# The same tasks in another hand-written order: a fused S5 scan and MLP kernel on one Trainium2 core

## The chip, the core and the metric

The kernel runs on one core of one Trainium2 chip (trn2). The metric is device time in microseconds (us), from start to end of one execution. Kernels are compared by the median of several runs on the same chip.

The core has a matrix engine (TensorE, called PE in the profile, with its weight loads as PEld), a vector engine (VectorE, DVE), an activation engine (ScalarE, ACT), a general engine (GpSimd, POOL) and a queue that only issues transfers here (SyncE, SP). Each engine takes its instructions strictly in the order in which the program lists them. An instruction that has to wait for a semaphore therefore holds up everything behind it on its engine.

## The reference

Input `x` is one sequence of 2048 rows with 448 channels, bf16. It is normalised twice (a layernorm of a layernorm feeds the MLP), goes through a complex diagonal recurrence (S5) and through an MLP of width 1792, and both meet in a gate:

```python
xn = layernorm(x)                                        # over the 448 channels
# A: S5. 448 complex states, one decay Lam_bar per state
Lam_bar = exp(exp(log_dt) * (Lambda_re + 1j * Lambda_im))
Bu      = xn @ B_bar.T ;  h[t] = Lam_bar * h[t-1] + Bu[t]     # t = 0..2047
s       = 2 * real(h @ C.T) + xn * Dskip
# B: MLP on the layernorm of xn, gate
m   = gelu_tanh(layernorm(xn) @ w1 + b1) @ w2 + b2
out = x + s * silu(m)
```

## The kernel before

**Tiling.** The 2048 rows are cut into four groups of 512 (`NG = 4`, g = 0 to 3), each of two blocks of 256 rows; a block holds its even and odd rows as two halves of 128 partitions. Two steps of the recurrence are folded into one, so that the scan of a group runs over 256 positions, and the two outputs of a pair come from two prepared matrices, `CZ` and `CQ`.

**What each group does.** Statistics and normalisation (`ln_stats`, L399; `ln_scale`, L478 to L488; `ln_apply`, L499 on DVE or L500 on ACT) give `xn` for the scan and `xm` for the MLP. Both are turned by transposing transfers that SP issues (L83); only the first group's `xm` is transposed on PE (L460) and copied from PSUM (L417). The first MLP layer `mm1_run` (matmuls L801) writes pairs of PSUM banks, and ACT's Gelu (L805) empties them: there are three pairs, so PE can be at most three pairs ahead of ACT. The second layer `mm2` (L828) needs the Gelu outputs; DVE adds its bias (L831). The scan's input `bu` (L729) goes to ACT or DVE (L417), then `ssm` on DVE: products (L744 to L748), scans (L753, L755), products back (L771 to L775) into `h_sb`. The outputs `ym` (L871, L874, L877) use one PSUM bank, number 7, for groups 0 to 2, which DVE must read (L885 or L888, or L883) before the next `ym` may write it. The result is added and stored (L891, SP).

**What runs once.** At the start a few tiny vectors of the S5 parameters are worked out in some eighty small operations on 128x4 or 128x16 elements (L534 to L592; a sine polynomial of ten chained steps, L545 to L551), then tables of sines (`tables`: DVE L624 to L631, ACT L640), then the mixed matrices `LB` and `CQ`, `CZ` (`combine`, L658 to L661) and `M0` (L712, L697, and their PSUM reads L417, L718, L705). PE begins with matmuls on constants whose result nobody reads (`dummies`, L422). ACT loads four function tables after its first (L443, L614, L618, L614 again near the end).

**What sets the order.** The body of the kernel only records tasks: 633 of them, each with an engine, its reads and its writes. Some are recorded with two possible engines (`either`, `small`, `copy`, `combine`, `ln_apply`). Then `Plan.emit` takes two lists of numbers written out at the top of the file:

```python
for k in SECOND:
    self.tasks[k].choose(1)
order = [self.tasks[k] for k in ORDER]
```

`SECOND` names the tasks that go to their second engine, and `ORDER` the sequence in which all tasks are handed to the engines. The waits are derived from reads and writes after that, so any order that respects them computes the same thing. No scheduler and no due times stand behind the lists when the program is built: the order on each engine is what `ORDER` says.

Of the kernel before, what the change touches and what calls it, by code (L numbers as in the profile page):

```python
# [159 lines left out]


ORDER = [int(k) for k in """
# [17 lines left out]
""".split()]  # L180
SECOND = [int(k) for k in """
45 53 54 61 63 66 69 74 76 83 112 130 133 158 160 162 163 165 177 184 185 187 189 190 220 222 224 226 228 230 238 248 249 258 266 268 331 362 364 365
384 400 401 436 447 468 480 482 487 491 499 501 502 504 510 528 529 609 612 627
""".split()]


# [834 lines left out]
```

## Time and profile before

| | |
|---|---|
| time of the kernel before | 153.37 us, median of 3 runs (153.15 to 153.41) |
| span of the profiled execution, first to last instruction | 151.8 us |
| time of the three runs beyond that span | 1.6 us |
| busy: PE / DVE / ACT / POOL | 147.1 / 127.6 / 99.0 / 42.1 us |
| instructions: PE / DVE / ACT / POOL | 1127 / 267 / 183 / 101 |
| granted TensorE clock | 1.00 |

The profile gives no time of its own beside the span: what lies around the profiled execution is taken as the difference of the median and the span. In rows of the timeline the first number is the start in us from the span's start, the second the length of the piece, then engine, source line, operation, what is written and read, and how many instructions were merged; the bracket behind a row gives the idle time before it and what ended it. A row of a group of instructions has "busy us, mean ns of one | idle us before". A row of the windows gives the stretch, its length, and the busy time of each engine with its number of instructions.

### The profile page before, as it was taken

What the parts mean: (1) busy time and instruction counts of PE and PEld (TensorE: products, weight loads), DVE (VectorE), ACT (ScalarE), POOL (GpSimd) and SP (SyncE); (2) the same over time, 40 slices, a digit from 0 to 9 for tenths busy, and PEclk for the clock granted to TensorE, in tenths of its full rate; (3) what the DMA queues carried; (4) which work ended last, traced back from release to release, by engine and by line L of the source; (5) the groups of instructions that cost most, each with busy time, mean ns of one, the idle gap of its engine ahead of it and who ended that gap; (6) DMA issues with size and microseconds to landing.
All of it is one profiled execution on the core that took longest, in us unless ns stands there. A gap on an engine that the chain in (4) does not pass through costs nothing.

```text
span 151.8 us, 2974 instructions
## 1 busy us (share of the span) xinstructions
PE 147.1 (97%) x1127; PEld 86.6 (57%) x1127; DVE 127.6 (84%) x267; ACT 99.0 (65%) x183; POOL 42.1 (28%) x101
## 2 busy tenths in 40 slices
PE   7899999999999999999999999999999999999992
PEld 7785755454566577545444556764454666555551
DVE  2874999999978979999999996379968726999984
ACT  3888996988789559997898610463579834067400
POOL 5376827153020920010456006200072031000201
PEclk9999999999999999999999999999999999999999
DMA  4999999989997300700003032610331001100022
GB/s 116 262 305 390 266 202 138 219 152 133 165 261 180 65 0 0 138 0 4 0 0 63 4 60 45 154 60 4 60 101 23 0 4 57 64 0 0 4 84 98
DMA packets 31236, 14.73 MB, mean 97 GB/s; under 512 B 24752, under 2 KB 30774, under 8 KB 31222
## 3 DMA queue, kind: packets, MB, share of 16 engines
q1 hardware_dynamic: 30912, 14.26, 41.8%
q0 software_dynamic: 160, 0.23, 1.0%
q8 instruction: 9, 0.15, 0.4%
q10 hardware_dynamic: 150, 0.05, 0.1%
q14 instruction: 5, 0.04, 0.1%
HBM read 6.89 MB, written 1.84 MB: 57 GB/s over the span
## 4 chain that ended last, share of the span: by engine, by line
PE 80%; DVE 9%; DMA 4%; SPq 4%; issue 2%
PE psum L828 23%; PE psum L801 22%; PE psum L729 14%; PE psum L871 13%; DMA x_all<-in_A_x_dram 4%; PE psum L874 4%; SPq L84 4%; PE psum L712 3%; DVE xn_sb L499 2%; DVE lnst L399 1%; DVE s_w L628 1%; PE psum L877 1%; DVE o L831 1%; PE psum L697 1%; DVE tmp L891 1%
## 5 line engine op out<-in xcount | busy, mean ns | idle before, releaser
L801 PE MATMUL psum<-xn2T,w_sb 64*128 64x512 bf16 (+1 forms) x462 | 44.6, 345 | 0.3 <-ACT xn2T L417 0.2
L828 PE MATMUL psum<-w_sb,gT 128*128 128x448 bf16 x224 | 44.5, 353 | 0.2 <-DVE o L831 0.2
L805 ACT ACTIVATE gT<-psum,b1f 128x512 bf16<-128x512 f32 (+1 forms) x66 | 35.9, 625 | 10.4 <-PE psum L801 10.2
L801 PEld LDWEIGHTS psum<-xn2T,w_sb 64*128 64x128 bf16 x462 | 24.1, 109 | 19.8 <-ACT gT L805 2.3
L828 PEld LDWEIGHTS psum<-w_sb,gT 128*128 128x128 bf16 x224 | 21.5, 98 | 20.7 <-DVE o L831 0.6
L417 ACT ACTIVATE u_sb<-psum 128x512 bf16<-128x512 f32 (+2 forms) x22 | 10.5, 478 | 23.0 <-PE psum L729 22.7
L729 PE MATMUL psum<-xnT,BT 128*128 128x256 bf16 x196 | 24.0, 273 | 0.0
L729 PEld LDWEIGHTS psum<-xnT,BT 128*128 128x128 bf16 x196 | 18.9, 98 | 5.4 <-issue 1.1
L891 POOL TENSOR_TENSOR tmp<-t,x_all 128x448 bf16<-128x448 bf16 x5 | 5.2, 1032 | 33.1 <-DVE t L888 30.7
L753 DVE TENSOR_TENSOR_SCAN s_w<-dk,vs 128x774 f32<-128x774 f32 x8 | 14.0, 1760 | 0.1
L500 ACT ACTIVATE xn_sb<-x_all,lnw 128x448 bf16<-128x448 bf16 (+2 forms) x21 | 13.0, 662 | 1.2 <-DVE xn_sb L499 1.1
L417 ACT ACTIVATE vs<-s_w 64x256 bf16<-64x256 f32 (+2 forms) x16 | 10.9, 681 | 2.6 <-DVE s_w L753 1.5
L871 PE MATMUL psum<-CZ,h_sb 128*128 128x448 bf16 x56 | 11.9, 352 | 0.0
L871 PE MATMUL psum<-CQ,h_sb 128*128 128x448 bf16 (+2 forms) x54 | 10.5, 332 | 0.0
L399 DVE BATCH_NORM_STATS2 lnst<-x_all 128x6 f32<-128x448 bf16 x12 | 7.1, 617 | 3.4 <-DMA x_all<-in_A_x_dram 3.4
L831 DVE TENSOR_TENSOR o<-psum,b2bc 128x448 f32<-128x448 f32 x16 | 9.7, 614 | 0.2
L871 PEld LDWEIGHTS psum<-CZ,h_sb 128*128 128x128 bf16 x56 | 5.4, 98 | 4.7 <-DVE lnmv L405 0.4
L871 PEld LDWEIGHTS psum<-CQ,h_sb 128*128 128x128 bf16 x54 | 5.1, 98 | 4.0 <-DVE t L885 0.4
L874 PE MATMUL psum<-M,xnT 128*128 128x448 bf16 x32 | 7.4, 352 | 0.0
L480 POOL TENSOR_TENSOR lnw<-lnw,mhalf 128x8 f32<-128x8 f32 x3 | 7.2, 2404 | 0.3
L883 DVE TENSOR_TENSOR Cr<-psum,xd 128x448 f32<-128x448 f32 x7 | 4.3, 620 | 3.5 <-PE psum L877 3.4
L499 DVE TENSOR_SCALAR xn_sb<-x_all,lnw 128x448 bf16<-128x448 bf16 (+2 forms) x19 | 6.9, 396 | 0.0
(160 smaller groups left out, 189.1 us busy)
## 6 DMA issues: line engine op xcount, KB each, us to landing
out_dram<-tmp SPq DMA_DIRECT2D x7, 224.0 KB, 2.0
x_all<-in_A_x_dram SPq DMA_DIRECT2D x3, 448.0 KB, 4.0
w_sb<-in_B_w_dram SPq DMA_DIRECT2D x3, 448.0 KB, 8.4
w_sb<-in_B_w_dram SPq DMA_DIRECT2D x3, 384.0 KB, 4.8
vs<-in_A_C_re_dram SPq DMA_DIRECT2D x1, 392.0 KB, 11.6
Bn<-in_A_B_im_dram SPq DMA_DIRECT2D x1, 336.0 KB, 10.2
Bn<-in_A_B_re_dram SPq DMA_DIRECT2D x1, 336.0 KB, 10.5
vs<-in_A_C_im_dram SPq DMA_DIRECT2D x1, 336.0 KB, 10.8
```

Source lines behind the costliest of these rows:

```text
L399: dve([lambda e, b=b, par=par, q=q: e.bn_stats(lnst[:, q, :], x_all[:, 2 * g + b, par, :])], [f"x{2 * g + b}"] , [f"st{q}"], 0.62, prio)
L417: kb.either(("act", [lambda e, o=o, i=i: e.activation(o, i, ACT.Copy) for o, i in pairs]), ("dve", [lambda e, o=o, i=i: e.tensor_copy(o, i ...
L499: on = [("dve", [lambda e, o=o, i=i: e.tensor_scalar(o, i, rs, nb, op0=ALU.mult, op1=ALU.add) for o, i in parts], 0.4, 0.12), ("act", [lam ...
L500: ("act", [lambda e, o=o, i=i: e.activation(o, i, ACT.Identity, bias=nb, scale=rs) for o, i in parts], 0.75, 0.2)]
L729: fns = [lambda e, r=r, m=m, d=d: e.matmul(psum[:, 4, r * NK:(r + 1) * NK], BT[:, m, d, :], xnT[:, gx, d, :], start=(d == 0), stop=(d == 6 ...
L753: dve(lambda e, so=so, vi=vi: e.tensor_tensor_scan(so, dk[:].rearrange("p i c -> p (i c)"), vi, 0.0, ALU.mult, ALU.add), ["v", "vl", "dk", ...
L801: return lambda e: e.matmul(view(bk[k]), w1_sb[rows, d, fcol(2 * j + k)], rhs[rows, d, :, :], start=not second and n == 0, stop=second and ...
L805: act([lambda e, k=k: e.activation(gT[:, gb, 2 * j + k, :].rearrange("p (r c) -> p r c", r=2)[:, :, cols], view(bk[k]), ACT.Gelu_apprx_tan ...
L828: fns = [lambda e, fi=fi: e.matmul(psum[:, bk, 0:D], gT[:, gb, fi, q * 128:(q + 1) * 128], w2_sb[:, fi, :], start=(fi == 0), stop=(fi == N ...
L831: dve(lambda e: e.tensor_tensor(o2[:, fb, :], psum[:, bk, 0:D], b2bc[:], ALU.add), [f"ps{bk}", "b2bc"], [f"oo{fb}"], 0.62, prio - 76)
L871: fns = [lambda e, k=k: e.matmul(psum[:, bk, c0:c1], h_sb[:, hb, k, k0:k0 + 128], cm[:, k, c0:c1], start=(k == 0), stop=False) for k in ra ...
L874: fns += [lambda e, d=d: e.matmul(psum[:, bk, c0:c1], xnT[:, gx, d, xs], M0[:, d, c0:c1], start=False, stop=(d == 3)) for d in range(4)]
```

## The change

Two lists are replaced and nothing else. `ORDER` holds the same 633 numbers in another sequence. `SECOND` goes from 60 to 78 entries. SP's 23 loads at the start keep their order.

Counted by engine, 46 tasks with 65 instructions come to DVE: 30 from POOL (43 instructions: most of the parameter arithmetic, among it the wrap L542 to L544 and the ten steps of the sine polynomial, two `De` products L610, a few small steps of the scan's carry L764 to L769, an `xd` product L847 and four result additions L891) and 16 from ACT (22 instructions: the copy of the first transposed half L417, normalisations L500, PSUM copies L417 of `bu` and `M0`, one product L658, and two copies L417 of the last but one scan). Twenty tasks with 22 instructions leave DVE: 11 to POOL (small ones, `xd` products and two result additions) and 9 to ACT (the absolute value L631, which becomes an Abs at L630, normalisations and PSUM copies). DVE's program grows from 267 to 310 instructions, ACT's shrinks by 11 and POOL's by 32.

Of the new sequence, engine by engine:

- PE: thirteen of the constant matmuls now stand together ahead of the second set of transposes (L460) instead of around it. Six matmuls of the first `mm2` (L828) stand among the first group's L801, ahead of its last five pieces; before they followed them. Four `M0` and `bu` pieces and two `mm2` of group 1 change places; two `mm2` of group 2 change places; one `ym` of group 2 goes ahead of an `mm2` of group 3.
- DVE: the parameter steps taken over stand between the first normalisations, the PSUM copies of the transposed second block and the statistics of group 1 (L399). Two of the four L628 pieces stand ahead of the normalisation of group 1 instead of behind it. From there on, DVE's tasks are interleaved differently throughout.
- ACT: the Abs (L630) stands ahead of the last three Gelu pairs of group 0.
- SP: the two transposes of `xm` of group 1 are exchanged, and three of the four transposes of `Cr` stand ahead of those of `xn`.

```diff
 ORDER = [int(k) for k in """
-0 13 19 47 9 16 18 20 14 1 94 26 17 95 91 27 92 21 15 24 48 4 96 12 108 93 90 109 97 104 103 25 105 99 22 98 49 50 55 5 51 65 106 2 110 100 111 107 29
-101 112 30 56 28 52 114 23 54 32 53 131 57 117 128 31 118 113 121 170 115 33 46 132 168 133 129 39 130 34 66 171 253 250 102 119 155 40 123 251 252
...
+47 16 9 13 19 0 24 18 17 15 20 14 10 4 26 1 2 25 27 94 21 95 91 96 22 48 92 108 29 93 99 109 49 90 30 50 104 55 103 97 32 65 106 56 3 110 105 5 111 66
+100 8 33 12 98 107 101 112 51 46 114 28 52 102 113 54 64 23 39 118 128 53 131 117 40 57 115 171 119 155 41 58 132 42 129 169 116 31 121 38 67 170 123
...
 SECOND = [int(k) for k in """
-45 53 54 61 63 66 69 74 76 83 112 130 133 158 160 162 163 165 177 184 185 187 189 190 220 222 224 226 228 230 238 248 249 258 266 268 331 362 364 365
-384 400 401 436 447 468 480 482 487 491 499 501 502 504 510 528 529 609 612 627
+45 51 53 54 57 58 60 62 63 64 66 67 69 70 71 72 73 74 75 76 77 78 79 83 84 86 107 112 130 133 158 162 184 185 186 188 190 220 222 224 228 230 238 244
+248 258 263 265 266 334 345 352 353 354 361 362 364 376 379 400 402 403 449 450 468 469 480 482 487 495 502 516 525 526 572 612 619 627
```

30 rows, old and new, of the table ORDER are left out of this document.

## The prediction

> **What bounds the kernel now.** I read the page first: busy times, the slices, the shares of the chain.
>
> ```profile
> PE 147.1 (97%) x1127; PEld 86.6 (57%) x1127; DVE 127.6 (84%) x267; ACT 99.0 (65%) x183; POOL 42.1 (28%) x101
> ...
> PE   7899999999999999999999999999999999999992
> ...
> DVE  2874999999978979999999996379968726999984
> ...
> PE 80%; DVE 9%; DMA 4%; SPq 4%; issue 2%
> ```
>
> PE has no pause in any slice between the first microseconds and the last ones, and holds 80% of the chain. DVE is the second: full through most of the first two thirds. So there are two questions. Where does the new order let PE start or pack better, and where does it make PE wait for DVE, which gets 43 instructions more? PE's own timeline, in its groups:
>
> ```profile
> 0.83 2.93 PE L422 MATMUL psum<-const-bfloat16-1.0 128*128 128x128 bf16 x26 [0.83 <-PEq L1006]
> ...
> 6.85 2.50 PE L801 MATMUL psum<-xn2T,w_sb 64*128 64x256 bf16 x42 [0.19 <-ACT xn2T L417]
> ...
> 9.84 9.26 PE L801 MATMUL psum<-xn2T,w_sb 64*128 64x256 bf16 x126
> 19.03 8.12 PE L828 MATMUL psum<-w_sb,gT 128*128 128x448 bf16 x42
> 27.33 2.82 PE L828 MATMUL psum<-w_sb,gT 128*128 128x448 bf16 x14 [0.18 <-DVE o L831]
> 30.08 10.11 PE L801 MATMUL psum<-xn2T,w_sb 64*128 64x512 bf16 x90
> ...
> 79.62 1.06 PE L801 MATMUL psum<-xn2T,w_sb 64*128 64x512 bf16 x8
> 80.61 1.31 PE L871 MATMUL psum<-CQ,h_sb 128*128 128x448 bf16 x6
> ...
> 141.92 1.30 PE L871 MATMUL psum<-CQ,h_sb 128*128 128x448 bf16 x6
> ```
>
> Little is left to win. The one group that runs below its rate is the 126 matmuls at 9.84: by the code 28 have 512 columns, which take 10.11/90 = 0.112 us each in group 1, and 98 have 256, by width 0.056. That makes 8.6 us against 9.26. So 0.6 us are waits for Gelu, hidden in "busy"; the 42 before (2.50 against 2.35) hide 0.15, and 0.18 stands at 27.33: a reserve of 0.9 to 1.0.
>
> **What DVE has to carry.** The windows between three milestones: the last normalisation for group 1's MLP, the last `CQ`, and the first `ym` result (L885).
>
> ```profile
> 0.00:22.79 22.79, 21.13 (x254) 15.58 (x255) 16.17 (x60) 18.60 (x42) 12.81 (x47) 1.00 0.94 257
> 22.79:47.05 24.26, 24.08 (x180) 12.62 (x178) 22.52 (x57) 20.03 (x32) 7.35 (x22) 1.00 1.06 182
> 47.05:80.35 33.30, 33.30 (x250) 19.28 (x247) 31.77 (x60) 27.15 (x53) 9.44 (x15) 1.00 0.17 33
> ```
>
> DVE is idle 6.6, 1.7 and 1.5 us in these. The moved operations are priced by their twins, in the timelines of POOL and of DVE and in the groups by form:
>
> ```profile
> 14.30 0.21 POOL L545 TENSOR_SCALAR ang<-ang 128x16 f32<-128x16 f32 x1
> ...
> 17.95 0.22 POOL L551 TENSOR_TENSOR ang<-ang 128x16 f32<-128x16 f32 x1
> ```
>
> ```profile
> 17.65 0.16 DVE L478 TENSOR_SCALAR lnw<-lnmv 128x4 f32<-128x4 f32 x1
> ...
> 19.92 0.17 DVE L488 SCALAR_TENSOR_TENSOR lnw<-lnmv,lnw 128x8 f32<-128x8 f32 x1
> ```
>
> ```profile
> L891 POOL TENSOR_TENSOR tmp<-t,x_all 128x448 bf16<-128x448 bf16 x5 | 5.2, 1032 | 33.1 <-DVE t L888 30.7 <-DMA out_dram<-tmp 2.4
> ```
>
> ```profile
> L891 DVE TENSOR_TENSOR tmp<-t,x_all 128x448 bf16<-128x448 bf16 x10 | 3.8, 386 | 0.1
> ```
>
> The sine polynomial is ten chained steps, 3.9 us on POOL (first and last row). DVE's own ten-step chain (L478 to L488) takes 2.44 us, so I take 2.4 for it there. Other small chained steps cost 0.15 to 0.17, a result addition 0.39 instead of 1.03. Over the kernel this brings about 17 us to DVE and takes 6 to 7 away, so its busy time should end near 138 us, of a span near 155.
>
> **Part 1, the start: a gain of 0.6.** The first L801 start about 0.35 us later, for two reasons: the thirteen constant matmuls stand ahead of the second transposes, and the copy of that half goes to DVE behind the statistics. On the other hand six L828 (8.12/42 = 0.19 each, 1.2 us in all) now run inside the stretch where PE waits for Gelu. They fill the reserve of about 1.0, which less the 0.35 leaves 0.6: I take the end of the first group's `mm2` at 29.5 instead of 30.1. Bounds: 0.9 gained, 0.4 lost.
>
> **Part 2, the second Gelu table: a loss of 1.4.** DVE's timeline at the start, ACT's groups, ACT's timeline:
>
> ```profile
> 0.88 0.17 DVE L323 MEMSET dk<- 4x128 uint32 x1 [0.88 <-PEq L1006]
> 2.89 0.63 DVE L431 BATCH_NORM_STATS2 lnst<-x_all 128x6 f32<-128x448 bf16 x1 [1.85 <-DMA x_all<-in_A_x_dram]
> ```
>
> ```profile
> L833 ACT ACTIVATE g_sb<-o 128x448 bf16<-128x448 f32 x8 | 4.3, 571 | 3.1 <-DVE o L831 3.1
> L614 ACT ACT_TABLE_LOAD x2 | 2.6, 1283 | 0.1
> L640 ACT ACTIVATE WT<-s_w,sgn 128x256 bf16<-128x256 f32 (+1 forms) x3 | 2.2, 718 | 0.1
> L640 ACT ACTIVATE WT<-s_w 128x768 bf16<-128x768 f32 x2 | 1.7, 843 | 0.9 <-DVE s_w L631 0.9
> ...
> L658 ACT ACTIVATE tmp<-Bn,cw 128x448 f32<-128x448 bf16 x1 | 0.7, 669 | 0.0
> ```
>
> ```profile
> 19.37 2.30 ACT L805 ACTIVATE gT<-psum,b1f 128x256 bf16<-128x256 f32 x6
> ...
> 32.94 3.58 ACT L805 ACTIVATE gT<-psum,b1f 128x512 bf16<-128x512 f32 x6
> ```
>
> Up to the last normalisation for group 1, DVE had 16.2 us of work. The new list adds 4.8 of moved steps and 1.8 of pieces pulled ahead (two L628, one L831), and loses 0.7: 22.1. Some 2.7 us at the very start cannot be filled (0.88 and 1.85), so it ends at 25 instead of 22.8. The L628 that the Abs needs stands 5.3 us of work earlier, at 19.5. In the new ACT list everything behind the Abs waits for that, and then runs in a row: Abs 1.2 (a 768-wide table takes 0.84, by width 1.12 for 1024), three Gelu pairs 2.4, two normalisation pieces 1.2 (an estimate; a whole one takes less than a Silu and a half), table 1.3, four Silu 2.3, `tmp` 0.7, five sine tables 3.9, table 1.3: 14.3, and 0.1 between them. The second Gelu set is ready at 33.9 instead of 32.9, although PE comes earlier. PE has 42 matmuls until it needs its first banks back: 29.5 + 42 x 0.112 = 34.2. It gets them at 33.9 + 1.3 = 35.2, and once more about 0.3 late in the next rotation. PE loses 1.3 to 1.4 here, and stands 0.8 behind the old order. Bounds: 0 (if ACT keeps to its old times) and 2.5 (if DVE reaches that L628 a microsecond later).
>
> The transposes of group 1 hide (SP's timeline, and the table of transfers with its median time to landing):
>
> ```profile
> 21.67 3.21 SPq L83 DMA_TRANSPOSE xn2T<-xn_sb  x2
> ```
>
> ```profile
> xn2T<-xn_sb SPq DMA_TRANSPOSE x6, 3.2
> ```
>
> SP issues them at about 24.5 and 26 instead of 21.7 and 23.3, and they land 3.2 us (the median) later, near 29.2, where PE asks at 29.5. The cover is thin: without it they cost up to a microsecond, which is in the range.
>
> **Part 3, `M0` of the third column: a loss of 0.5.** The timelines of DVE and PE:
>
> ```profile
> 62.96 0.28 DVE L718 TENSOR_TENSOR M<-psum,s_w 128x128 bf16<-128x128 f32 x1
> ```
>
> ```profile
> 63.94 0.94 PE L697 MATMUL psum<-CQ,Bn 128*64 128x448 bf16 x7
> ```
>
> Before, DVE freed the bank at 63.24, 0.7 us ahead of L697. In the new list that L718 stands behind the first scan, two normalisations that came from ACT and a `tmp`. I take 0.5 of wait, between 0 and 1.5.
>
> **Part 4, the first `ym`: a loss of 1.4.** It writes bank 7, and the next `ym` has to wait for DVE's L885.
>
> ```profile
> 46.96 0.68 DVE L661 SCALAR_TENSOR_TENSOR CQ<-Cr,cw,tmp 128x448 bf16<-128x448 bf16 x1
> ...
> 79.73 0.62 DVE L885 SCALAR_TENSOR_TENSOR t<-psum,g_sb 128x448 bf16<-128x448 f32 x1
> ```
>
> From the last `CQ` to L885, DVE was busy 31.8 of 33.3 us. The new list adds 4.2 (a `bu` copy, two normalisations, `M0` and carry pieces, a `tmp`) and 1.5 pulled ahead of it (among it an L831), and takes 2.4 away: 35.1. With the same 1.5 of waits, and `CQ` at 46.9 as before (three microseconds more work, but DVE's early idle time is filled), L885 ends at 83.5. PE, 1.3 late by then, asks at 80.6 + 1.3 = 81.9, so it waits 1.6; I take 1.4, since a later PE also gives DVE's waits back in part. Bounds 0 and 3.
>
> **Part 5, the last scan: a loss of 0.5.**
>
> ```profile
> 141.37 0.29 DVE L775 TENSOR_TENSOR h_sb<-pa 128x256 bf16<-128x256 bf16 x1
> ```
>
> Its last piece ends at 141.66, 0.26 us before PE uses it at 141.92. Between L744 and this piece the new list puts 0.8 us more work (an L888, an L891, an L883 come in, an L836 and an L891 go out). That passes the margin by 0.5. The last results behind PE keep their length.
>
> **The sum.** -0.6 + 1.4 + 0.5 + 1.4 + 0.5 = 3.2 us, on a profiled span of 151.8: 155.0. The three runs' median lies 1.6 above that span; with the same surroundings, 153.37 + 3.2 = 156.6.
>
> **Rivals.** *The waits hide (152.7).* Parts 2 to 5 are all differences between DVE or ACT times that I add up and a need of PE. If DVE works its mixed list off about 2 us faster by each milestone, they vanish and part 1 is left: 153.37 - 0.6. For it: a small DVE step that waits for nothing before it may take less than the 0.16 I gave it. Against it: the added work is 5.9 us up to the first milestone and 3.3 from the second to the third, and the idle time of the two later windows only 3.2 together. Chance 0.12.
>
> *DVE's debt lands on `M0` (159.6).* In the new PE list the first `M0` follows its `mm2` directly, without a `bu` between, so `CQ` is wanted about 1.5 us sooner. If DVE does not fill its early idle time and `CQ` ends at 50 instead of 47, PE waits 2 to 3 us there more, and part 4 is unchanged: 156.6 + 3. For it speaks that DVE is full from 22.8 on (22.5 of 24.3). Chance 0.2.
>
> *PE starts at half its rate (157.5).* The first 26 constant matmuls take 2.93/26 = 0.113 us each, twice what 128 columns cost later (two 64-row L801 of 256 columns run side by side in 2 x 0.060, so 128 columns of the whole array cost 0.06). In the new list PE has nothing to do between the parameter matmuls and the first transposes, about half a microsecond (an estimate from the places in the lists), just when the rate changed. If it changes only after the thirteen others, the start of L801 moves 0.9 us: 17 matmuls of 128 columns at 0.053 more each. [...] Chance 0.15.
>
> *No change to be seen*, by chance of the terms: 0.03.
>
> **How the numbers follow.** The forecast has 0.5, the rivals 0.12, 0.2, 0.15 and 0.03. A measurement of this kernel can tell about 0.2% (0.3 us) from no change. Faster 0.12, same 0.03, slower 0.85. The range leaves out the fast rival and what lies above the slow one: 153.3 (parts 3 to 5 gone and part 2 at half, 153.37 - 0.6 + 0.7) to 160.0.
>
> **What would show it.** DVE busy 136 to 140, POOL near 30. The Gelu group after L618 starts 0.5 to 2 us later than 32.94, and the 43rd L801 of group 1 waits for it. PE shows idle or stretched groups before L697 and between the first L874 and the second L871. A first group of L828 that ends before 30 shows part 1 right. I am wrong if PE's groups from 40 to 140 keep their old distances, or if the largest wait stands where I see none, above all at group 1's transposes.

## The result: 1.7% slower, and the profile after

| | before | after |
|---|---|---|
| time, median of 4 runs each | 153.39 us (153.15 to 153.68) | 155.88 us (155.80 to 155.95) |
| ratio, with its 95% interval | | 1.0167 (1.0152 to 1.0182) |
| span of the profiled execution | 151.8 us | 154.1 us |

The change costs 2.5 us, 2.3 of them in the two spans. The runs of one kernel can lie at two levels, as 4 of the 17 runs of the kernel before that were taken beside e11_best did (154.8 to 155.1, the others 153.1 to 153.6), and no run of that upper level of the kernel before was traced. The forecast was 156.6, between 153.3 and 160.0. The total lies in that range. Its make-up was not right, as the page of the changed kernel begins to show (busy times, the slices of PE and of DVE, the shares of the chain):

```profile
PE 147.9 (96%) x1127; PEld 88.3 (57%) x1127; DVE 136.0 (88%) x310; ACT 92.8 (60%) x172; POOL 31.7 (21%) x69
...
PE   7799999999999999999999999999999899999992
...
DVE  2799998799997999999999899779999946999984
...
PE 55%; DVE 29%; ACT 6%; POOL 4%; issue 3%; DMA 1%; DVEq 0%; ACTq 0%
```

DVE now holds 29% of the chain instead of 9%, and its busy time of 136.0 is what the new list was said to bring. PE has a second weak slice at the start and one that ends at 123 us. PE's timeline gives the places:

```profile
4.92 0.61 PE L460 MATMUL psum<-ident,xn_sb 128*128 128x128 bf16 x4 [0.63 <-DVE xn_sb L453]
5.32 1.59 PE L422 MATMUL psum<-const-bfloat16-1.0 128*128 128x128 bf16 x13
6.70 0.63 PE L460 MATMUL psum<-ident,xn_sb 128*128 128x128 bf16 x4
...
7.95 2.61 PE L801 MATMUL psum<-xn2T,w_sb 64*128 64x256 bf16 x34 [0.33 <-DVE cw L534]
...
18.06 1.31 PE L828 MATMUL psum<-w_sb,gT 128*128 128x448 bf16 x6
...
21.39 9.63 PE L828 MATMUL psum<-w_sb,gT 128*128 128x448 bf16 x50
30.95 10.00 PE L801 MATMUL psum<-xn2T,w_sb 64*128 64x512 bf16 x90
...
68.85 9.93 PE L801 MATMUL psum<-xn2T,w_sb 64*128 64x512 bf16 x90 [0.38 <-DMA xn2T<-xn_sb]
...
82.24 1.31 PE L871 MATMUL psum<-CQ,h_sb 128*128 128x448 bf16 x6 [0.29 <-DVE t L885]
...
122.94 1.48 PE L871 MATMUL psum<-CZ,h_sb 128*128 128x448 bf16 x7 [0.62 <-DVE h_sb L775]
...
144.18 1.30 PE L871 MATMUL psum<-CQ,h_sb 128*128 128x448 bf16 x6
```

PE's lateness is the start of a group here less its start before. The first L801 come 1.10 late (7.95 against 6.85). By 17 us it is 1.52, because the first L801 run slowly too: up to 9.0 us each pair of them takes 0.213 us, and 0.109 behind that. The six hoisted L828 (the matmuls of the first `mm2` that now stand among the L801) win back 0.65, so the second `mm1` starts 0.87 late (30.95 against 30.08). It stays near 0.85 up to 68 us. Then three waits come: before the first L801 of group 2, before the second `ym`, and before the first `ym` of group 2, where lateness goes from 1.47 to 2.25. The last `ym` groups are 2.26 late (144.18 against 141.92).

### The profile page after: what moved, and what is told of

Read it like the earlier page. It is cut to its first block, busy times and chain, and to the rows that moved or that the text cites. A ratio compares the mean times of both kernels' runs of the same rounds, so it can differ in the third digit from the quotient of the medians.

```text
span 154.1 us, 2968 instructions
## 1 busy us (share of the span) xinstructions
PE 147.9 (96%) x1127; PEld 88.3 (57%) x1127; DVE 136.0 (88%) x310; ACT 92.8 (60%) x172; POOL 31.7 (21%) x69
## 4 chain that ended last, share of the span: by engine, by line
PE 55%; DVE 29%; ACT 6%; POOL 4%; issue 3%; DMA 1%; DVEq 0%; ACTq 0%
PE psum L828 17%; PE psum L801 15%; PE psum L871 10%; PE psum L729 7%; DVE s_w L753 5%; PE psum L874 3%; DVE vs L417 2%; DVE h_sb L773 2%; ACT tmp L658 2%; POOL lnw L480 1%; ACT u_sb L417 1%; DMA x_all<-in_A_x_dram 1%; DVE pb L772 1%; DVE pa L744 1%; DVE CZ L661 1%
## 5 line engine op out<-in xcount | busy, mean ns | idle before, releaser
L801 PE MATMUL psum<-xn2T,w_sb 64*128 64x512 bf16 (+1 forms) x462 | 44.7, 348 | 0.7 <-DMA xn2T<-xn_sb 0.4
L805 ACT ACTIVATE gT<-psum,b1f 128x512 bf16<-128x512 f32 (+1 forms) x66 | 36.1, 624 | 14.3 <-PE psum L801 13.8
L828 PE MATMUL psum<-w_sb,gT 128*128 128x448 bf16 x224 | 44.5, 353 | 0.0
L801 PEld LDWEIGHTS psum<-xn2T,w_sb 64*128 64x128 bf16 x462 | 25.2, 109 | 19.4 <-issue 2.5
L828 PEld LDWEIGHTS psum<-w_sb,gT 128*128 128x128 bf16 x224 | 21.7, 98 | 19.9 <-issue 0.8
L417 ACT ACTIVATE u_sb<-psum 128x512 bf16<-128x512 f32 (+2 forms) x19 | 9.3, 492 | 16.9 <-PE psum L729 16.7
L417 ACT ACTIVATE vs<-s_w 64x256 bf16<-64x256 f32 (+2 forms) x12 | 8.1, 681 | 5.4 <-DVE s_w L755 4.0
L478 POOL TENSOR_SCALAR lnw<-lnmv 128x4 f32<-128x4 f32 x3 | 1.5, 498 | 44.2 <-DVE lnmv L405 42.7
L831 DVE TENSOR_TENSOR o<-psum,b2bc 128x448 f32<-128x448 f32 x16 | 9.9, 616 | 0.8 <-PE psum L828 0.7
L500 ACT ACTIVATE xn_sb<-x_all,lnw 128x448 bf16<-128x448 bf16 (+2 forms) x16 | 9.9, 657 | 0.4 <-POOL lnw L482 0.3
L833 ACT ACTIVATE g_sb<-o 128x448 bf16<-128x448 f32 x8 | 4.4, 571 | 8.3 <-DVE o L831 8.3
L891 POOL TENSOR_TENSOR tmp<-t,x_all 128x448 bf16<-128x448 bf16 x3 | 3.1, 1044 | 28.6 <-DVE t L885 25.1
L499 DVE TENSOR_SCALAR xn_sb<-x_all,lnw 128x448 bf16<-128x448 bf16 (+2 forms) x24 | 7.8, 360 | 0.0
L399 DVE BATCH_NORM_STATS2 lnst<-x_all 128x6 f32<-128x448 bf16 x12 | 7.4, 614 | 0.0
## 6 DMA issues: line engine op xcount, KB each, us to landing
vs<-in_A_C_re_dram SPq DMA_DIRECT2D x1, 392.0 KB, 10.9
vs<-in_A_C_im_dram SPq DMA_DIRECT2D x1, 336.0 KB, 11.8
```

Source lines behind the costliest of these rows:

```text
L399: dve([lambda e, b=b, par=par, q=q: e.bn_stats(lnst[:, q, :], x_all[:, 2 * g + b, par, :])], [f"x{2 * g + b}"] , [f"st{q}"], 0.62, prio)
L417: kb.either(("act", [lambda e, o=o, i=i: e.activation(o, i, ACT.Copy) for o, i in pairs]), ("dve", [lambda e, o=o, i=i: e.tensor_copy(o, i ...
L499: on = [("dve", [lambda e, o=o, i=i: e.tensor_scalar(o, i, rs, nb, op0=ALU.mult, op1=ALU.add) for o, i in parts], 0.4, 0.12), ("act", [lam ...
L500: ("act", [lambda e, o=o, i=i: e.activation(o, i, ACT.Identity, bias=nb, scale=rs) for o, i in parts], 0.75, 0.2)]
L801: return lambda e: e.matmul(view(bk[k]), w1_sb[rows, d, fcol(2 * j + k)], rhs[rows, d, :, :], start=not second and n == 0, stop=second and ...
L805: act([lambda e, k=k: e.activation(gT[:, gb, 2 * j + k, :].rearrange("p (r c) -> p r c", r=2)[:, :, cols], view(bk[k]), ACT.Gelu_apprx_tan ...
```

## The experiments

All kernels below leave the computation whole. They are moves in the lists `ORDER` and `SECOND`, shown as each engine's own list; `dummies(n)` are the constant matmuls L422. Since the moment at which PE reaches its upper rate varies (128 columns every 0.056 us instead of every 0.107; it stands at about 9 us in the changed kernel and before 4.8 us in e6_trans, with the same head of PE's list), the time alone can't judge a part of 0.5 us; the one trace of each kernel is read too. The row "before" gives the medians of the batches that the others were compared with. The last three columns are read from PE's timelines (start of the first L801, end of the first `mm2`, start of the last `ym` groups).

| kernel | median (range), us | ratio to before | first L801 | `mm2` ends | last `ym` |
|---|---|---|---|---|---|
| before | 153.25 to 153.39 | 1 | 6.85 | 30.15 | 141.92 |
| after | 155.88 (155.80 to 155.95) | 1.0167 (1.0152 to 1.0182) | 7.95 | 31.02 | 144.18 |
| e1_warm | 155.19 (155.03 to 155.88) | 1.0121 (1.0096 to 1.0147) | 6.91 | 31.10 | 144.24 |
| e2_cold | 155.26 (155.14 to 155.92) | 1.0131 (1.0104 to 1.0157) | 7.83 | 31.87 | 143.65 |
| e3_hoist | 154.16 (154.06 to 155.70) | 1.0073 (1.0042 to 1.0105) | 6.85 | 30.69 | 142.48 |
| e4_sb3 | 155.24 (154.52 to 155.47) | 1.0101 (1.0074 to 1.0129) | 8.10 | 31.43 | 143.80 |
| e5_pool | 154.99 (154.12 to 155.52) | 1.0106 (1.0081 to 1.0131) | 7.94 | 31.17 | 143.52 |
| e6_trans | 155.70 (155.20 to 156.26) | 1.0154 (1.0128 to 1.0181) | 6.81 | 29.82 | 143.52 |
| e7_warm | 155.65 (155.43 to 155.69) | 1.0148 (1.0129 to 1.0166) | 7.47 | 30.49 | 143.96 |
| e8_all | 155.52 (155.23 to 155.81) | 1.0140 (1.0120 to 1.0161) | 7.53 | 30.58 | 144.06 |
| e9_relief | 155.88 (155.21 to 156.72) | 1.0154 (1.0100 to 1.0208) | 7.87 | 30.92 | 143.56 |
| e10_all | 153.96 (153.66 to 154.32) | 1.0019 (0.9989 to 1.0048) | 6.90 | 30.14 | 141.91 |
| e11_best | 154.15 (153.90 to 154.61) | 1.0032 (0.9998 to 1.0067) | 7.08 | 30.08 | 142.40 |

### The start of PE, from both sides

```diff
 e1_warm: the changed kernel, PE's head (90 = dummies(8), 109 and 105 = transposes)
-48 109 90 103 106 105 111
+48 90 109 103 106 105 111
 e2_cold: the kernel before, PE's head
-48 90 109 103 105 106 111
+48 109 90 103 105 106 111
```

> The changed kernel with one group of PE moved: the eight constant matmuls of L422 stand ahead of the first four transposes again, as in the kernel before, so that PE has something to do between 4.3 and 4.9 us. Theory (the pause at 4.3 put off the step of the matmul rate from 4.85 to 9.0 us, and that is the 1.5 us by which the whole first group is late): the rate steps at 4.9, the first L801 starts at about 7.0 instead of 7.95, and the group at 11.50 about 1.4 earlier. Of these 1.4, DVE's list lets only a part through to the end, since DVE is busy without a pause from 48 to 85: the time falls by 0.3 to 1.2 us, to 154.7 to 155.6. Rival A (the late second transposes and the copy on DVE cost the start, not the rate): the first L801 moves by less than 0.4. Rival B (losses simply add): the time falls by 1.4 to 1.5, to 154.4.

> The kernel before with one group of PE moved: the eight constant matmuls of L422 stand behind the first four transposes, as in the changed kernel. Theory (rate): the pause at 4.3 to 4.9 comes back, constant matmuls and transposes run at 0.107 us until about 9, the first L801 starts 0.7 to 1.1 later, the first mm1 group ends 1.2 to 1.5 later, and nothing behind it gives it back: 154.5 to 154.9. Rival A (order alone, rate not concerned): the first L801 starts up to 0.4 later and the time is 153.4 to 153.8.

PE's timeline of e2_cold, the kernel before with one group moved:

```profile
4.85 0.61 PE L460 MATMUL psum<-ident,xn_sb 128*128 128x128 bf16 x4 [0.78 <-DVE xn_sb L453]
5.25 1.38 PE L422 MATMUL psum<-const-bfloat16-1.0 128*128 128x128 bf16 x11
...
7.83 3.60 PE L801 MATMUL psum<-xn2T,w_sb 64*128 64x256 bf16 x42 [0.28 <-ACT xn2T L417]
```

One moved group of constant matmuls leaves PE idle for 0.78 us. The eleven behind it take about 0.107 us each (from the first start to the next group, 1.17 us), and the 42 L801 take 3.60 us where they took 2.50 before. In the starts of single matmuls the step to the upper rate stands at 10.2 us, against 4.85 in the kernel before. The first `mm1` is 2.07 late; 0.34 comes back ahead of the last group of the first `mm2`, where the kernel before had a wait of its own, and from there the kernel runs as before, 1.73 late to the end. No run out of five was under 155.14. So the moved group and its pause are enough to cost 1.7 us. The mechanism of the theory held and its price was too low (154.5 to 154.9), with the step at 10.2 instead of 9.

The other way round is less clean. Four runs of e1_warm took 155.03 to 155.42, which is 0.5 to 0.85 less than after. The traced one is the fifth, 155.88. Its windows, with the granted clock in the column behind POOL's time:

```profile
6.00:8.00 2.00, 1.66 (x23) 1.48 (x22) 1.64 (x11) 1.89 (x4) 0.72 (x5) 0.75 0.89 210
8.00:10.00 2.00, 2.00 (x22) 2.00 (x20) 1.90 (x10) 1.07 (x3) 0.73 (x3) 0.50 1.05 284
10.00:12.00 2.00, 2.00 (x31) 1.56 (x29) 1.80 (x8) 1.31 (x5) 1.83 (x3) 0.90 0.98 336
```

Here the rate stepped up before 3.95 us, and PE then idled 0.33, 0.27 and 0.34 us between 4.4 and 6.6. From about 7.0 to 10.4 the clock was halved again (0.75, 0.50 and 0.90 in the three windows), and this run's lateness and time are those of the changed kernel. So the array's rate decides the start, as the theory said, in a way that depends on the run. The kernel e6_trans below shows the same: its head is that of the changed kernel, and in the traced run the rate had stepped up by 4.8 us in spite of the pause. Its six runs stand at two levels, three at 155.2 to 155.3, the traced one among them, and three at 156.1 to 156.3. If the upper level is that of a late step, which no trace shows, the start is worth 0.9 us at the end in this kernel, not the 1.5 seen at 17 us.

### The hoisted matmuls alone

```diff
 e3_hoist: the kernel before, PE's list (271 = the six L828)
-147 145 151 144 148 150 153 276 271 272
+147 145 271 151 144 148 150 153 276 272
```

> The kernel before with the six L828 of the first half of o0 pulled ahead of the last five groups of the first mm1, as in the changed kernel, and nothing else. Theory (they fill waits for Gelu): the last five groups of mm1 run without the three gaps of 0.13 us, and the end of the first mm2 comes 0.3 to 0.6 earlier than 30.15; the time is 152.8 to 153.1. Rival (PE's gain is taken back at the next wait for ACT or DVE, such as the one of 0.18 us at 27.33): 153.3 to 153.4.

Neither time came (the median is 154.16): the first `mm2` ends 0.54 later. The rival had the right place, the wait for DVE at 27.33, and too low a price. PE's timeline, then DVE's:

```profile
27.87 2.82 PE L828 MATMUL psum<-w_sb,gT 128*128 128x448 bf16 x14 [0.51 <-DVE o L831]
```

```profile
24.84 1.23 DVE L631 SCALAR_TENSOR_TENSOR s_w<-s_w 128x1024 f32<-128x1024 f32 x1
25.98 0.45 DVE L659 TENSOR_SCALAR tmp<-Bn,cw 128x448 f32<-128x448 bf16 x1
26.46 0.68 DVE L661 SCALAR_TENSOR_TENSOR Bn<-Bn,cw,tmp 128x448 bf16<-128x448 bf16 x1
...
27.23 0.59 DVE L831 TENSOR_TENSOR o<-psum,b2bc 128x448 f32<-128x448 f32 x1
```

The gaps in `mm1` stayed, since there ACT runs three normalisation pieces between the Gelu pairs. The last group of `mm2` then waits for a bank that DVE frees only behind its work on the sine table. In the changed kernel the normalisation pieces are gone from that place and this L831 runs at 25.76, as soon as its matmuls end. By these rows the gain of 0.65 belongs to the three edits together; no run has the hoist with one of the other two alone.

### The wait at 122.9: what stretched DVE

```diff
 e4_sb3: the changed kernel; 526 = sb3 copy (L417) of group 2
-DVE: 534 526 535 536       ACT: 546 549 454
+DVE: 534 535 536           ACT: 546 549 526 454
 e5_pool: the changed kernel, POOL's list (495 = L891, 507 and 508 = L847)
-528 531 507 529 495 530 508 589
+528 531 529 530 589 495 507 508
```

> The changed kernel with one copy back on ACT, the sb3 copy (L417) of group 2 that DVE ran from 119.51 to 121.14, now behind a Gelu pair on ACT. Theory (DVE's list of group 2 ends 0.6 us too late for the ym of group 2): the last step of that scan ends at about 121.2, PE's idle 0.62 us at 122.9 vanishes, and the time falls by 0.6 to 0.75, to 155.1 to 155.3. Rival (the wait sits in what DVE gets earlier, and the copy comes as late on ACT): PE still waits 0.4 or more there, 155.6 to 155.9.

> The changed kernel with three POOL operations moved behind another one of POOL, L769: the result addition L891 of 119.61 and the two L847 of 117.36 and 121.16, which nobody needs before 125. DVE's list is untouched. Theory (beside these POOL operations DVE's own are stretched: L773 at 117.80 took 1.79 us against 0.97 of its twin at 72.38, the sb3 copy 1.63 against 1.24 on ACT, L774 1.30 against 0.42): DVE ends that scan 1.5 us or more earlier than 122.80, PE's 0.62 us at 122.9 vanishes, and the time falls by 0.6 to 0.75 to about 155.2. Rival (DVE is late there by its list alone): the wait keeps at least 0.4, 155.7 to 155.9.

DVE's timeline of the changed kernel, POOL's beside it, and DVE's in e5_pool:

```profile
117.80 1.78 DVE L773 TENSOR_TENSOR h_sb<-pa,pb 128x1536 bf16<-128x1536 bf16 x1
119.51 1.63 DVE L417 CAST vs<-s_w 128x256 bf16<-128x256 f32 x3
121.17 1.30 DVE L774 TENSOR_TENSOR pa<-vs,WT 128x512 bf16<-128x512 bf16 x1
122.51 0.29 DVE L775 TENSOR_TENSOR h_sb<-pa 128x256 bf16<-128x256 bf16 x1
```

```profile
117.36 1.41 POOL L847 TENSOR_TENSOR xd<-xn_sb,dbc 128x448 bf16<-128x448 bf16 x1
...
119.61 1.07 POOL L891 TENSOR_TENSOR tmp<-t,x_all 128x448 bf16<-128x448 bf16 x1
...
121.16 1.03 POOL L847 TENSOR_TENSOR xd<-xn_sb,dbc 128x448 bf16<-128x448 bf16 x1
```

```profile
117.93 0.95 DVE L773 TENSOR_TENSOR h_sb<-pa,pb 128x1536 bf16<-128x1536 bf16 x1
118.81 0.90 DVE L417 CAST vs<-s_w 128x256 bf16<-128x256 f32 x3
119.74 0.42 DVE L774 TENSOR_TENSOR pa<-vs,WT 128x512 bf16<-128x512 bf16 x1
120.19 0.29 DVE L775 TENSOR_TENSOR h_sb<-pa 128x256 bf16<-128x256 bf16 x1
```

Both theories held. In e4_sb3 and in e5_pool PE has no wait at that place, and the 0.78 by which lateness rises there in the changed kernel is not added in either. In e5_pool nothing was taken from DVE: the same four pieces take 2.5 us instead of 5.0, only because three operations of POOL, which nobody needed before 125, ran later. L774 shows it best: 0.42 us alone, and 1.30 when it began 0.01 us behind a POOL operation of 1.03. L773 and L774 have two inputs and the copies L417 one, and all are stretched: 1.78 us against 0.95, 1.30 against 0.42, 1.63 against 0.90 for the three copies. L836, at 117.27 in the changed kernel, is not: it takes 0.61 us beside the first L847, and 0.61 in e5_pool. What POOL's operations do to DVE's, and which pairs are stretched, is not shown.

### The transposes of group 2, and whether waits add

```diff
 e6_trans: the changed kernel, DVE's list (376, 379 = L499; 471 = L399)
-471 343 241 332 344 346 379 376 244
+343 241 376 332 379 344 346 471 244
```

> The changed kernel with the two DVE pieces of group 2's normalisation (L499, at 62.31 and 62.80) two microseconds earlier in DVE's list and a statistic (L399 of 58.37) later in exchange, so that the transposes go out earlier. Theory (DVE has been full since 48 and its L885 at 81.57 does not depend on PE's time, so the two waits do not add): PE's 0.4 us at 68.85 vanishes, the wait at the second ym, 82.24, grows from 0.3 to 0.6 or 0.7, and the time stays at 155.8 to 155.9. Rival (the waits add): 0.4 less, 155.4.

PE's timeline, and one row of ACT's:

```profile
4.83 0.40 PE L460 MATMUL psum<-ident,xn_sb 128*128 128x128 bf16 x4 [0.78 <-DVE xn_sb L453]
5.06 0.92 PE L422 MATMUL psum<-const-bfloat16-1.0 128*128 128x128 bf16 x13
...
6.81 2.25 PE L801 MATMUL psum<-xn2T,w_sb 64*128 64x256 bf16 x34
```

```profile
35.36 4.72 PE L801 MATMUL psum<-xn2T,w_sb 64*128 64x512 bf16 x42 [0.26 <-ACT gT L805]
63.37 0.94 PE L697 MATMUL psum<-CQ,Bn 128*64 128x448 bf16 x7 [0.16 <-DVE M L718]
81.60 1.31 PE L871 MATMUL psum<-CQ,h_sb 128*128 128x448 bf16 x6 [0.47 <-DVE t L885]
122.29 1.48 PE L871 MATMUL psum<-CZ,h_sb 128*128 128x448 bf16 x7 [0.61 <-DVE h_sb L775]
```

```profile
19.21 1.06 ACT L630 ACTIVATE s_w<-s_w 128x1024 f32<-128x1024 f32 x1 [1.35 <-DVE s_w L628]
```

The wait for the transposes is gone, and the one at the second `ym` grew from 0.29 to 0.47, less than the 0.6 or 0.7 of the theory. The theory's reason, that L885 does not depend on PE's time, did not hold. The work ahead of it is the same, but it came 0.64 us earlier, in a run in which DVE had waited less for PE (0.3 instead of 0.7 us ahead of its first L831). DVE's timeline in the changed kernel, then in e6_trans:

```profile
81.57 0.62 DVE L885 SCALAR_TENSOR_TENSOR t<-psum,g_sb 128x448 bf16<-128x448 f32 x1
```

```profile
80.93 0.62 DVE L885 SCALAR_TENSOR_TENSOR t<-psum,g_sb 128x448 bf16<-128x448 f32 x1
```

PE asks 0.82 us earlier here and DVE is done 0.64 earlier, which is the growth of the wait. How much of it PE's start made, and how much the moved pieces, this trace can't tell. The times speak against the rival all the same: neither the lower three runs (those of e1_warm lie at 155.03 to 155.42) nor the upper three (156.1 and more, against 155.88) show a gain of 0.4.

This trace is worth more, because here PE started in time. It was 1.5 us ahead of the changed kernel at 10 us and wins 0.44 at the transposes, but only 0.66 are left at the end. The rest went into waits that the late start had covered: for DVE's copies of the next transposes (0.3 at 11.8), for the Gelu set (0.26), for `M0` (0.16), for a PSUM bank that DVE's L705 gives free at 68.5 (0.26, inside the L801 behind the transposes), and more at the second `ym`.

### Mending everything at once

```diff
 e7_warm: the changed kernel, PE's head, and longer dummies
-48 109 90 103 106 105 111     dummies 8, 3, 2
+48 90 109 103 105 106 111     dummies 11, 7, 8
 e8_all: e7_warm with the edits of e5_pool and e6_trans, and
-ACT: 177 152 154 149 (177 = Abs)   DVE: 394 320 393 431 (320 = L831, 431 = L885)
+ACT: 152 154 149 177               DVE: 394 431 320 393
```

> The changed kernel with PE's head in the order of before and with 13 more constant matmuls in it (11, 7 and 8 instead of 8, 3 and 2), so that PE has no pause over 0.2 us from 3.8 to 6.6. Theory (rate): the rate steps by 5 and stays, the first L801 starts at 6.9 to 7.1, the group at 11.50 comes 1.4 earlier, and the end of the first mm2 is 29.6. Of these 1.4 a part is lost again where DVE and ACT are now late: at the Gelu pairs behind the second Gelu table (PE's 43rd L801 of group 1, 35.50 before, waits 0.3 to 0.7) and at the second ym. Time 154.8 to 155.2. Rival (all of the start comes through): 154.4 or less. Rival (the start does not matter): 155.7 or more.

> The changed kernel with all that the traces point to: the warm head of PE with the 13 constant matmuls more, the Abs (L631) behind the three Gelu pairs of the first group, the two L499 of group 2 earlier, the L885 of the first ym ahead of an L831, and the three POOL operations of group 2 later. Theory (start 1.4 back, the wait at 122.9 gone, but DVE stays full between 48 and 94 and holds PE up at the second ym or at the ym of group 1): 153.6 to 154.4. Rival (the waits were all there was, and the hoisted L828 win their 0.6): 152.7 to 153.0, faster than before.

Both missed. In e7_warm the added constant matmuls ran at the low rate (0.107 us apart up to 6.3 us) and pushed the transposes back. The first L801 start at 7.47, and 0.4 more is lost at 12.5 us, where PE waits for DVE's copies of the next block's transposes. In e8_all, PE's timeline and ACT's:

```profile
36.47 4.73 PE L801 MATMUL psum<-xn2T,w_sb 64*128 64x512 bf16 x42 [0.32 <-ACT gT L805]
...
84.26 2.82 PE L828 MATMUL psum<-w_sb,gT 128*128 128x448 bf16 x14 [0.59 <-ACT gT L805]
```

```profile
82.47 0.58 ACT L835 ACTIVATE th<-o 128x448 f32<-128x448 f32 x1 [1.35 <-DVE o L831]
82.96 1.25 ACT L805 ACTIVATE gT<-psum,b1f 128x512 bf16<-128x512 f32 x2
```

The L885 moved ahead of an L831 takes the wait from the second `ym`. But ACT's L835 waits for that L831, and the Gelu pair that the next `mm2` needs is queued behind it. The wait went round through ACT and became 0.59.

### Less work for DVE, and the best version

```diff
 e9_relief: the changed kernel, out of SECOND
-334 352 353 354 361 376 379 402 403   (on DVE)
+ACT: 375 378 376 384 379 336 313      POOL: 352 353 354 402 403
 e10_all: e9_relief, e5_pool, PE's head of before with dummies 8, 6, 5, and DVE
+31 133 130 (copies of transposes)   174 176 175 (L628)   475 474 (L405)
 e11_best: e10_all, PE's first mm1 groups
-114 113 118 117 115 132 129 121
+114 117 113 121 118 115 132 129
```

> The changed kernel with nine operations between 51 and 98 us back on the engines that ran them before: two copies (L417 of 51.09 and 66.85) and two normalisation pieces (L500 instead of L499, 62.31 and 62.80) on ACT, five small carry steps (L764 to L769) on POOL; together 4.2 us less for DVE there, 3.2 of them before the first L885. The lists keep their order, but for three of ACT's places. Theory (DVE is the bound between 48 and 94, which is why a wait that is taken away in one place came back in the next): PE's waits at 68.85 (0.4) and at 82.24 (0.3) are both gone, DVE is idle before the L885, and the end comes 0.5 to 0.9 earlier than in the changed kernel for the same start of PE; the wait at 122.9 stays. Time 155.0 to 155.4 with a late rate step, some 0.9 less with an early one. Rival (order alone makes the waits, whatever DVE carries): one of the two waits stays, and less than 0.3 is won.

> The kernel of the nine operations, and with it the three POOL operations of group 2 later, PE's head in the order of before with six constant matmuls more (6 and 5 instead of 3 and 2), DVE's two copies of block 1's transposes (L417 of 11.74 and 12.16) and two of the L628 for the Abs ahead of other work, and the aggregation L405 of 86.60 at 79.3. Theory (start on time, hoisted L828, and no wait on DVE left): the first L801 starts at 6.9, the first mm2 ends at 29.5 to 29.8, no wait of PE over 0.2 us from 12 to 140, span 151.0 to 151.6: 152.6 to 153.2, faster than the kernel before. Rival (DVE's list has other places that wait): 153.6 to 154.4.

> The kernel of the run before (all places mended), with PE's first six groups of L801 in the order of the kernel before: both groups of the second weight tile ahead of those of the first, whose weights landed at 7.60 there while PE asked at 7.2. Theory (the 0.6 us by which mm1 was still late at 12.14 were that wait and what followed): mm1 runs at the times of the kernel before, the hoisted L828 bring the end of the first mm2 to 29.5 to 29.8, the Gelu set follows since nothing holds ACT, and the time is 153.2 to 153.7, level with the kernel before or up to 0.3 faster. Rival (the next wait, for the Gelu pairs or a DVE result, takes it back): 153.9 to 154.1, as without it.

The groups of PE in e9_relief, with the idle time behind the bar:

```profile
L801 PE MATMUL psum<-xn2T,w_sb 64*128 64x512 bf16 (+1 forms) x462 | 44.7, 348 | 0.3 <-DVE cw L534 0.3
...
L871 PE MATMUL psum<-CQ,h_sb 128*128 128x448 bf16 (+2 forms) x54 | 10.5, 332 | 0.0
```

With 4.2 us less on DVE's list both waits are gone and the last `ym` comes 0.62 earlier than in the changed kernel, as the theory said. DVE was not idle right ahead of the L885, as I had expected: it reached it at 80.95 instead of 81.57, no earlier than in e6_trans, where nothing was taken from DVE. Part of what was taken away came back as a wait of DVE for ACT (DVE's timeline):

```profile
69.89 0.96 DVE L772 TENSOR_TENSOR pb<-vs,WT 128x1536 bf16<-128x1536 bf16 x1 [1.34 <-ACT vs L417]
```

In the changed kernel the same L772 starts at 70.00 after a wait of 0.31. So there ACT's copy sets the pace, and that DVE's load alone is the bound between 48 and 94 is not shown. The time does not show the gain. Its six runs lie 1.5 us apart, more than the part in question, so by time this run is inconclusive.

In e10_all PE has no wait over 0.1 us from 12 us on, its last groups start where they did before, and the ratio to the kernel before can't be told from 1 (0.9989 to 1.0048). But the runs of the kernel before that it is compared with reach from 153.13 to 155.12, with a median of 153.38, and none of the twelve runs of e10_all was under 153.66. So the forecast of 152.6 to 153.2 missed, and the time is the rival's. At the last `ym` nothing of the change's 2.26 us is left. The span is 0.4 longer than before all the same: 0.06 of it stand at DVE's last row, and what makes the rest, behind that row, is not shown. Nothing is won: the 0.65 of the hoisted matmuls went into a start that is still late. One row of PE's timeline:

```profile
7.74 1.71 PE L801 MATMUL psum<-xn2T,w_sb 64*128 64x256 bf16 x28 [0.31 <-DMA w_sb<-in_B_w_dram]
```

The new PE list asks for the first weight tile as its second group, and that tile landed at 7.60. Asking for it one group later (e11_best) removed that wait, and short ones took its place at 10.2 and 10.9 us, the second for a Gelu pair that ended at 10.82. The rival held, and no version tried is faster than the kernel before.

## Why the prediction was right, and where it was not

That a fuller and reordered list of DVE comes out as waits of PE at a few places is shown for three places, with 1.6 us together. Only one of them, the second `ym`, is in the sum, and the largest comes from POOL's operations beside DVE's and not from the length of DVE's list. DVE's busy time was to be near 138 and is 136.0, POOL's 31.7. The time rose by 2.5 instead of 3.2, and PE's last groups came 2.26 later. That the total is near is luck for the larger part: parts 2 to 5 were put 3.4 us too high together, and part 1 and what was not forecast 2.5 too low. (Two small sums are off as well: 153.37 - 0.6 is 152.8 and not 152.7, and with 0.7 more the range would begin at 153.5.)

- **Part 1, -0.6 forecast, +0.9 measured.** The step that failed is "the first L801 start about 0.35 us later". They start 1.10 later, and the first of them, up to 9.0 us, run at half rate (0.213 us a pair instead of 0.109). The rival on PE's start did happen and was given 0.15. Its price of 0.9 counted only constant matmuls and transposes; the slow L801 made it 1.5. The other half of the part held: the hoist won 0.65, though not by itself, as e3_hoist shows. With a start in time (e6_trans) the first `mm2` ends at 29.82 instead of the 29.5 forecast.
- **Part 2, +1.4 forecast, 0 measured.** The place on ACT was right, as e6_trans shows: the Abs waits 1.35 us for its L628 at 19.2, where the forecast had 19.5. What followed took 0.6 less than summed (13.7 from the start of the Abs to the Gelu set behind the table load L618, not 14.3), and `mm2` ended later than forecast. So the set came in time for the first rotation of banks and cost 0.26 in the second. In the changed kernel PE was late enough to hide that too. The two terms were added as if they were independent; a late PE pays for a late ACT.
- **Part 3, +0.5 forecast, 0 measured;** 0.16 when PE is in time. The same cause.
- **Part 4, +1.4 forecast, 0.35 measured;** idle 0.29, and 0.47 in e6_trans. The place was right. L885 ended at 82.2, not 83.5: DVE was busy for 33.4 us from 47.0 to 82.2, where 35.1 had been summed.
- **Part 5, +0.5 forecast, 0 measured.** The last L775 ends 0.15 ahead of PE.
- **Not in the forecast: 1.2.** The transposes of group 2 (0.44), where only those of group 1 had been weighed, and the first `ym` of group 2 (0.78), less some 0.2 of small gains. The second is the largest wait of all that the change brought. Part 5 weighed the scan of the last group only, and all of DVE's work was summed with undisturbed durations, which left no place for what POOL's operations beside it cost.

Of the signs named in advance, DVE's and POOL's busy times came, the Gelu group behind L618 started 0.8 later (33.75), and PE idled ahead of the second `ym`. The others spoke against the make-up: the first group of L828 ended at 31.02 and not before 30, no L801 waited behind the second Gelu table, none stood idle before L697, and the largest wait stood where none was seen.

The rival on PE's start is borne out in part. The step of the rate stands at 4.85 (before), about 9 (after) and 10.2 us (e2_cold). Six traces have a pause of 0.63 to 1.00 us ahead of the first transposes. In five of them (after, e2_cold, e4_sb3, e5_pool, e9_relief) four transposes still take 0.63 us at 6.4 to 6.9 us, where the kernel before took 0.40 at 5.67; in the sixth, e6_trans, with a pause of 0.78 us, the upper rate was there at 4.83. So such a pause goes with a late step, but not in every run. For the way back there is one trace: in e1_warm the clock went back to half from about 7.0 to 10.4 us after three pauses of together 0.94 us. In e3_hoist three pauses of together 0.74 us, and in e6_trans one of 0.28 us, did not bring the clock back. What sets the step, and which pauses are enough, is not shown.

## What to carry to other kernels

Terms that lie on one path did not add here: a wait early in the chain covered the later ones (in e6_trans 1.5 us gained by 10 us left 0.66 at the last `ym`). So each should be priced against the lateness that PE has by then, and a mended wait should be expected to come back at the next place where the loaded engine is late. Where a trace shows operations of VectorE stretched beside those of GpSimd, as at 117.8 us here (5.0 us for four pieces that take 2.5 in e5_pool), sum VectorE's list with the stretched durations, and move GpSimd work that nobody waits for out of VectorE's critical stretch. Keep TensorE's first microseconds free of pauses (the moved group of e2_cold, with its pause of 0.78 us, cost 1.7 us), but not with so much filler that it delays the work behind it, as in e7_warm (first L801 at 7.47 instead of 6.85), and judge a change there by several runs.

## What was not expected of the hardware

- The row of the granted clock shows 1.00 from 6 to 8 us in the changed kernel, while matmuls of 128 columns start 0.107 us apart, and 0.50 from 8 to 10 us in e1_warm at the same pace (22 L801 in 2 us there; 11 from 8 to 9 us in the changed kernel, where the row shows 1.00). So in these traces the row shows a clock that falls back, and not one that has not yet risen; the row of the changed kernel:

```profile
6.00:8.00 2.00, 1.67 (x21) 1.42 (x21) 1.04 (x8) 1.88 (x4) 0.41 (x4) 1.00 0.85 245
```

- Three operations of POOL, 3.5 us in all, made a chain of DVE 2.5 us longer (L773, the copies L417 and L774).
